# One copy of the 128-token chain behind each count of 192-token bodies; counting products in 64x64 blocks; the last copy over two engines

## The chip, the cores and the metric

The kernel runs on one core of one Trainium2 chip. The metric is the device time of one launch in microseconds (us), as the median of three runs.

## The reference

Sigmoid attention over 8 batches, 12 heads, 448 tokens and head size 64, then a mixture of 8 experts with one expert per token (3584 tokens, model width 768, hidden width 1024):

```python
scores = scale * np.matmul(q, k.transpose(0, 1, 3, 2)) - np.log(S)
attn = 1.0 / (1.0 + np.exp(-scores))
x = np.matmul(attn, v)                      # then (B*S, H*D)
logits = x @ w_gate
e_idx = np.argmax(logits, axis=1)
gate_w = softmax(logits)[np.arange(N), e_idx]
eom = 1.0 / (1.0 + np.exp(-(x @ w_output_gate)))
for e in range(E):
    mask = e_idx == e
    h = np.maximum(x[mask] @ w1[e], 0.0)
    out[mask] = gate_w[mask, None] * eom[mask, e, None] * (h @ w2[e])
```

## The kernel before, in words

**Attention** runs as 168 units (`attention`, from L858). A unit computes scores of 64 keys per head half (L898, matmuls on 64x64 blocks of TensorE), a sigmoid on ScalarE (L900) and, two units later, the products with v (L907, 64x64 blocks too), which gather in PSUM banks 4 to 7.

**Routing** (`route`) runs beside it for groups of 3, 2, 1, 1 and 1 batches. For each group it builds a one-hot matrix `oh` of tokens and experts and counts tokens: two TensorE products of 128x128 weights, `tri` for places within a chunk (L332) and `ones` for totals (L333). They go to one PSUM bank (`mm_ps`, bank 5; for the last group `mm_late`, bank 7), and ScalarE copies them out (L335). The counts give each token a row in the list of its expert, and GpSimd writes the lists by indirect DMA.

**Experts.** Each expert's tokens are cut into bodies: 256 tokens (`slot`), then a remainder as bodies of 192 (`wide_slot`) and of 128 tokens (`half_slot`). How many there are of each is known at run time only (`full`, `wide`, `part`, read at L1089 to L1091). A body multiplies its tokens by w1 (L644, L645, or L818 to L820 for 128 tokens), splits the hidden values in high and low parts, multiplies by w2 (L669 to L671), scales on ScalarE (L689, L850) and stores by indirect DMA (L691, L851). Weights of the next body are loaded by SyncE's queue (L587) and split by ScalarE (L600, L604) and VectorE (L601, L607).

The order of the bodies is written out by hand. The 256-token bodies behind the first are nested `If`s (L1102), the 192-token bodies a second nest (L1107), the 128-token bodies a chain (L1122 and L1127). Each nest leaves to one join, whatever its depth:

```python
for k in range(E):
    ctx.enter_context(tc.If(wide > k, label=f"wide{k}"))
    with tc.manual_schedule():
        self.wide_slot(k, hint("wide", wide, k, E))
```

`hint` marks, on TensorE alone, early in a body whether the next branch will be taken (a `BRANCH_PREFETCH_HINT`). Since the join can be reached from nine depths, each way out passes a landing block in which every engine waits for its own instructions and adds the counts of the bodies that did not run, so that all semaphores stand as if all had run; waits behind the join are against those sums. With the inputs timed here three 192-token and two 128-token bodies run.

The very last store is that of the last 128-token body: TensorE's second half of layer 2, ScalarE's scaled copy of 128x384 values (L850), the indirect DMA (L851).

Of the kernel before, what the change touches and what calls it, by code (L numbers as in the profile page):

```python
# [10 lines left out]
F32 = mybir.dt.float32  # L11
# [3 lines left out]
AF = mybir.ActivationFunctionType  # L15
ALU = mybir.AluOpType
# [7 lines left out]
E = 8  # L24
# [28 lines left out]
PLAIN = 6 * DF * 4 + 2 * XG + 8 * DM * 4  # L53


def r32(ap):
    return ap.bitcast(F32)


class Kernel:  # L60
# [20 lines left out]
    def memory(self):  # L81
        self.rounded = self.pool("rounded").tile([128, ROUNDED // 4], F32R, name="rounded")
        self.plain = self.pool("plain").tile([128, PLAIN // 4], F32, name="plain")
        ps = self.pool("psum", space=PSUM).tile([128, 8, 512], F32, name="ps")
        self.ps_s = [ps[:, 0:2], ps[:, 2:4]]
        self.ps_third = ps[:, 6:8]
        self.ps_o = [[ps[:, 4], ps[:, 5]], [ps[:, 6], ps[:, 7]]]
        self.mm_ps, self.mm_late = ps[:, 5], ps[:, 7]
        self.gp = ps[:, 6]
        self.psx = [ps[:, i].rearrange("p (d t) -> p d t", d=2) for i in (6, 7)]  # L90
        self.psh = [ps[:, i] for i in (0, 1, 2, 4, 5)]
        self.psy = [ps[:, i, 0:384] for i in (4, 5, 3, 6)]
        self.rot = {}

        c = self.carve
        w = c(0, 3, 2, 2, DF)
        self.w1s = [[w[:, d // 2, a, d % 2] for d in range(6)] for a in range(2)]
        self.w1p = [[w[:, k, a] for k in range(3)] for a in range(2)]
        self.xc = c(12 * DF * 4, 6, 2, TS)
        self.xs = [self.xc[:, :, i] for i in range(2)]  # L100

        self.w1r = c(0, 6, DF, dt=F32)
        o = 6 * DF * 4
        self.xg = c(o, 8, Q4, dt=F32)
        self.xT = c(o + XG, 6, TS, dt=F32)
        o += 2 * XG
        self.w2r = c(o, 8, DM, dt=F32)
        self.li = c(o, LROWS, 6, dt=F32)
        self.lr_e = [c(o + LROWS * 24 + i * 768, 192, dt=F32, parts=32) for i in range(2)]
        self.tmp_early = o + 4096  # L110
        self.step = c(o + 8192, B, 4, dt=F32)
        self.tokf = c(o + 8192 + 16 * B, NCH, 4, dt=F32)
# [146 lines left out]
    def route_tiles(self):  # L259
        rp, g = self.pool("route"), self.nc.gpsimd  # L260
        t = lambda n, shape, dt=F32: rp.tile(shape, dt, name=n)
        self.R, at = {}, [0]
        place = {3: 46080, 2: 53248}

        def early(name, dims):
            a = self.carve(at[0], *dims, dt=F32)
            at[0] += 4 * math.prod(dims)
            return a

        for k in sorted({n for _, n in GROUPS}):  # L270
            n = k * NCH
            at[0] = place.get(k)
            m = early if k > 1 else lambda name, dims: t(name, [128, *dims])
            R = self.R[k] = {
                name: m(name, dims)
                for name, dims in (("ahead", (E, n)), ("lg", (n, 32)), ("df", (n, E)), ("rk", (n, E)), ("sg", (3, n, E)),
                                   ("mf", (2, n)), ("t4", (n, 4)), ("t2", (n, 2)), ("posf", (n,)), ("den", (n,)),
                                   ("eom", (n,)), ("posi", (n,)), ("oh", (n * E // 2,)))}
            R["posi"] = R["posi"].bitcast(I32)
            R["oh"] = R["oh"].bitcast(BF16).rearrange("p (c e) -> p c e", e=E)  # L280
            lg = R["lg"].rearrange("p c x -> p (c x)")
            R["pc"], R["inc"], R["pos"] = (lg[:, n * E * i:n * E * j] for i, j in ((0, 2), (2, 3), (3, 4)))
            R["pos"] = R["pos"].rearrange("p (c e) -> p c e", e=E)
        g.memset(self.R[1]["ahead"], 1.0)
        g.memset(self.R[1]["ahead"][:, :, 0:1], 0.0)
        self.bad = t("bad", [128, NCH])
        for q in range(4):
            g.iota(self.bad[32 * q:32 * q + 32], pattern=[[32, NCH]], base=-QT, channel_multiplier=1,
                   allow_small_or_imprecise_dtypes=True)
        g.tensor_scalar(self.bad, self.bad, 0.0, float(OOB), ALU.is_ge, ALU.mult)  # L290
# [8 lines left out]
    def route(self, b, nb):  # L299
        nc = self.nc  # L300
        g, v = nc.gpsimd, nc.vector
        tt = g.tensor_tensor
        n = nb * NCH
        R = self.R[nb]
        mf, sg, pc, inc = R["mf"], R["sg"], R["pc"], R["inc"]
# [3 lines left out]
        by_c = lambda t: t.rearrange("p (c e) -> p c e", e=E)  # L309
        by_e = lambda t: t.rearrange("p (e c) -> p c e", e=E)  # L310
# [16 lines left out]
        oh = R["oh"]  # L327
        nc.scalar.activation(sg[:, 0], R["df"], AF.Sigmoid)
        nc.scalar.activation(sg[:, 1], R["df"], AF.Sigmoid, scale=-1.0)
        nc.scalar.activation(sg[:, 2], R["lg"][:, :, E:16], AF.Sigmoid)  # L330
        ps = self.mm_ps[:, 0:2 * n * E]
        nc.tensor.matmul(by_c(ps[:, 0:n * E]), self.tri, oh, start=True, stop=True)  # L332
        nc.tensor.matmul(by_e(ps[:, n * E:]), self.ones, oh, start=True, stop=True)  # L333
        yield "places"
        nc.scalar.copy(pc, ps)  # L335
        den = R["den"]
        v.reciprocal(sg[:, 1], sg[:, 1])
        v.tensor_tensor(sg[:, 0], sg[:, 0], sg[:, 1], ALU.mult)
# [412 lines left out]
            out_offset=bass.IndirectOffsetOnAxis(ap=s["lq"][:, 0:1], axis=0),  # L751
            in_=y[:, 0:384], in_offset=None, bounds_check=2 * NT - 1, oob_is_err=False)

    def wide_slot(self, j, hint):
        cur = self.wide_lists(j)
        if j:
            self.load_held()
        nx = self.load_slot(self.tab_l, LATE_F + j + 1, self.wide_lists(j + 1))
        self.nc.gpsimd.drain()
        self.split_w2(0)  # L760
        for f in range(8):
            if f == 6:
                self.finish()
            self.layer1(f, n=WS)
            if f == 0:
                hint()
            if f:
                self.high_low(f - 1, HS)
            if f in (1, 3, 5):
                self.split_w2(f // 2 + 1)  # L770
        self.high_low(7, HS)
        self.high_w1(0)
        self.turn_x(nx)
        self.gather(self.wide_lists(j + 2))
        for k in range(3):
            self.split_x(nx, k)
        self.low_w1(0)
        self.split_w1(1)
        self.split_w1(2)
        self.layer2_q(cur, self.ys[0])  # L780
        self.load_w2(nx, (0, 2, 4))
        self.layer2(cur, 0, 0, self.ys[1], self.psy[1])
        self.layer2_due(cur, 0)
        k = LATE_F + j + 1
        self.nc.vector.tensor_copy(self.held, self.tab_l[0:1, 0:3:2, k])

    def half_slot(self, j, last):
        nc = self.nc
        nx, y = None, self.ys[j % 2]
# [19 lines left out]
        for n in range(2):  # L809
            c = slice(512 * n, 512 * n + 512)  # L810
            ps = self.take("h", self.psh)
# [15 lines left out]
        cur = dict(lt=self.ltb[:, j])  # L827
        pss = self.psy[0:2]
# [15 lines left out]
        for n in range(2):  # L844
            self.layer2_mm(pss[n], 0, n, range(4, 8))
            if not last:
                self.layer2_out(pss[n], cur, 0, n, y)
                continue
            c = slice(384 * n, 384 * n + 384)
            nc.scalar.activation(y[:, c], pss[n], AF.Copy, scale=r32(cur["lt"][:, 0, 1:2]))  # L850
            nc.gpsimd.indirect_dma_start(  # L851
                out=self.outs[n].rearrange("t (n c) -> (t n) c", n=2),
                out_offset=bass.IndirectOffsetOnAxis(ap=self.lth[:, j, n:n + 1], axis=0),
                in_=y[:, c], in_offset=None, bounds_check=2 * NT - 1, oob_is_err=False)
# [165 lines left out]
    def build(self, phases="abc"):  # L1020
        tc, nc = self.tc, self.nc
# [65 lines left out]
        for m in range(EARLY + LATE_MIN):  # L1087
            if m == EARLY + LATE_MIN - 1:
                full = nc.values_load(self.tot[0:1, 0:1], min_val=0, max_val=LATE_MAX)  # L1089
                wide = nc.values_load(self.tot[0:1, 1:2], min_val=0, max_val=E)  # L1090
# [5 lines left out]
        def hint(name, n, k, end):  # L1096
            def mark():
                if k + 1 < end:
                    tc.mark_branch_hint_location(f"{name}{k + 1}", hint=n > k + 1, engines=[ET.PE])
            return mark  # L1100

        with ExitStack() as ctx:  # L1102
            for k in range(LATE_MIN, LATE_MAX):
                ctx.enter_context(tc.If(full > k, label=f"full{k}"))
                with tc.manual_schedule():
                    self.slot(EARLY + k, hint=hint("full", full, k, LATE_MAX))
        with ExitStack() as ctx:  # L1107
            for k in range(E):
                ctx.enter_context(tc.If(wide > k, label=f"wide{k}"))
                with tc.manual_schedule():  # L1110
                    self.wide_slot(k, hint("wide", wide, k, E))
        def body(k, last):
            with tc.manual_schedule():
                self.half_slot(k, last)
            if not last:
                halves(k + 1)
# [7 lines left out]
            with first.Else():  # L1124
                body(k, False)

        with tc.If(part > 1) as more:  # L1127
            body(0, False)
        with more.Else():
            with tc.If(part > 0) as one:  # L1130
                body(0, True)
            with one.Else():
                with tc.manual_schedule():
                    self.finish()


@with_exitstack
# [34 lines left out]
```

## Time and profile before

| | us |
|---|---|
| median of 3 runs (lowest, highest) | 765.19 (764.56, 765.5) |
| the profiled execution | 764.83 |
| its span, first to last instruction | 763.0 |
| TensorE busy (share of the span) | 755.0 (99%) |
| VectorE busy | 494.3 (65%) |
| ScalarE busy | 482.3 (63%) |
| GpSimd busy | 319.7 (42%) |

The profile is of one execution. PE is TensorE's array, PEld its weight loads, DVE VectorE, ACT ScalarE, POOL GpSimd, SP SyncE. A q behind a name (PEldq, ACTq) is that engine's instruction queue: branches, events and waits run there, and it may be ahead of the engine. Lines such as L818 are the kernel's. TensorE's granted clock is 0.998 of full over the span.

### The profile page before, as it was taken

What the parts mean: (1) busy time and instruction counts of PE and PEld (TensorE: products, weight loads), DVE (VectorE), ACT (ScalarE), POOL (GpSimd) and SP (SyncE); (2) the same over time, 40 slices, a digit from 0 to 9 for tenths busy, and PEclk for the clock granted to TensorE, in tenths of its full rate; (3) what the DMA queues carried; (4) which work ended last, traced back from release to release, by engine and by line L of the source; (5) the groups of instructions that cost most, each with busy time, mean ns of one, the idle gap of its engine ahead of it and who ended that gap; (6) DMA issues with size and microseconds to landing.
All of it is one profiled execution on the core that took longest, in us unless ns stands there. A gap on an engine that the chain in (4) does not pass through costs nothing. (4 is left out here: it accounts for less than half of the span.)

```text
span 763.0 us, 15197 instructions
## 1 busy us (share of the span) xinstructions
PE 755.0 (99%) x5775; PEld 591.2 (77%) x5775; DVE 494.3 (65%) x918; ACT 482.3 (63%) x643; POOL 319.7 (42%) x400
## 2 busy tenths in 40 slices
PE   9999999999999999999999999999999999999996
PEld 5777754444434489899999999999999999889786
DVE  3333344345477579888887866858576685877783
ACT  5666657666687756566565665757566574675683
POOL 5000005502446477883643727255372734524611
PEclk9999999999999999999999999999999999999999
DMA  7463544536486450238857768511156856488691
GB/s 262 143 218 137 198 174 146 176 118 219 138 320 250 115 178 10 76 90 339 287 188 270 247 212 294 160 52 43 42 189 216 297 158 220 165 291 296 216 383 60
DMA packets 43648, 144.82 MB, mean 190 GB/s; under 512 B 5623, under 2 KB 7839, under 8 KB 42528
## 3 DMA queue, kind: packets, MB, share of 16 engines
q1 hardware_dynamic: 33872, 119.56, 44.9%
q0 software_dynamic: 9680, 24.07, 9.3%
q8 instruction: 49, 0.80, 0.4%
q14 instruction: 47, 0.39, 0.2%
HBM read 145.93 MB, written 23.06 MB: 221 GB/s over the span
## 5 line engine op out<-in xcount | busy, mean ns | idle before, releaser
L644 PE MATMUL ps<-rounded 128*128 128x512 f32 (+1 forms) x672 | 225.7, 385 | 0.7 <-PEq L1102 0.7
L900 ACT ACTIVATE a<-ps,bias_s 128x896 f32<-128x896 f32 x168 | 169.1, 1007 | 87.0 <-PE ps L898 86.4
L564 POOL DMA_INDIRECT plain<-x_dram,lxs x122 | 182.5, 1496 | 93.3 <-DVE plain L626 54.6
L898 PE MATMUL ps<-kqv 64*64 64x448 f32 x1344 | 193.9, 542 | 0.0
L907 PE MATMUL ps<-a,kqv 64*64 64x448 f32 x1344 | 192.1, 536 | 0.0
L645 PE MATMUL ps<-rounded 128*128 128x256 f32 (+1 forms) x672 | 183.9, 274 | 0.0
L669 PE MATMUL ps<-w2h,h 128*128 128x384 f32 x432 | 145.0, 336 | 0.0
L671 PE MATMUL ps<-w2h,h 128*128 128x384 f32 x432 | 144.5, 334 | 0.0
L670 PE MATMUL ps<-w2l,h 128*128 128x384 f32 x432 | 144.5, 334 | 0.0
L601 DVE TENSOR_TENSOR w2l<-plain,w2h 128x1536 fp32r<-128x1536 f32 x60 | 105.2, 1756 | 60.5 <-ACT w2h L600 60.5
L644 PEld LDWEIGHTS ps<-rounded 128*128 128x128 f32 x672 | 125.8, 187 | 23.6 <-issue 1.8
L645 PEld LDWEIGHTS ps<-rounded 128*128 128x128 f32 x672 | 127.3, 189 | 0.0
L898 PEld LDWEIGHTS ps<-kqv 64*64 64x64 f32 x1344 | 66.5, 134 | 60.0 <-issue 41.8
L907 PEld LDWEIGHTS ps<-a,kqv 64*64 64x64 f32 x1344 | 67.3, 133 | 57.8 <-issue 45.1
L607 DVE TENSOR_TENSOR rounded<-plain,rounded 128x2048 fp32r<-128x2048 f32 x44 | 98.9, 2285 | 2.9 <-ACT rounded L604 2.9
L652 ACT COPY gl<-ps 128x256 f32<-128x256 f32 (+1 forms) x112 | 40.4, 360 | 95.3 <-PE ps L645 89.5
L600 ACT CAST w2h<-plain 128x1536 fp32r<-128x1536 f32 x60 | 88.0, 1469 | 17.8 <-PE ps L943 4.8
L604 ACT CAST rounded<-plain 128x2048 fp32r<-128x2048 f32 x44 | 83.4, 1902 | 0.0
L669 PEld LDWEIGHTS ps<-w2h,h 128*128 128x128 f32 x432 | 81.1, 188 | 2.3 <-issue 1.8
L670 PEld LDWEIGHTS ps<-w2l,h 128*128 128x128 f32 x432 | 81.1, 188 | 0.1
L671 PEld LDWEIGHTS ps<-w2h,h 128*128 128x128 f32 x432 | 81.1, 188 | 0.0
L691 POOL DMA_INDIRECT out<-y,due x11 | 20.0, 1814 | 126.3 <-ACT gl L652 116.1
(259 smaller groups left out, 663.8 us busy)
## 6 DMA issues: line engine op xcount, KB each, us to landing
plain<-w SPq DMA_DIRECT2D x64, 768.0 KB
plain<-w SPq DMA_DIRECT2D x45, 1024.0 KB
kqv<-kqv SPq DMA_DIRECT2D x23, 1344.0 KB
x_dram<-xt SPq DMA_DIRECT2D x8, 1344.0 KB
plain<-w SPq DMA_DIRECT2D x6, 512.0 KB
plain<-x_dram,lxs POOLq DMA_INDIRECT x122, 5.3
kqv<-kqv SPq DMA_DIRECT2D x2, 448.0 KB
lst<-plain POOLq DMA_DIRECT2D x1, 726.0 KB
```

The costliest lines, as they stand in the source:

```text
L564: self.nc.gpsimd.indirect_dma_start(out=s["xg"][:, g], out_offset=None, in_=x4, in_offset=bass.IndirectOffsetOnAxis(ap=s["lx"][:, g:g + 1] ...
L600: self.nc.scalar.copy(hi, raw)
L601: self.nc.vector.tensor_tensor(lo, raw, r32(hi), ALU.subtract)
L607: self.nc.vector.tensor_tensor(self.w1p[1][k], self.w1r[:, 2 * k:2 * k + 2], r32(self.w1p[0][k]), ALU.subtract)
L644: nc.tensor.matmul(out, wh[d][:, c], both, start=(d == 0), stop=False)
L645: nc.tensor.matmul(ps[:, 0:n], wl[d][:, c], self.xc[:, d, 0, 0:n], start=False, stop=(d == 5))
L669: nc.tensor.matmul(ps, hh[:, f, tk], wh, start=(f == 0), stop=False)
L670: nc.tensor.matmul(ps, hh[:, f, tk], wl, start=False, stop=False)
L671: nc.tensor.matmul(ps, hl[:, f, tk], wh, start=False, stop=(f == 7))
L898: nc.tensor.matmul(ps[half[h], j, 0:S], kg[half[j], e, 1, o:o + 64], kg[half[j], e, 0], start=True, stop=True)
L900: nc.scalar.activation(at[u % 4], ps[:, :, 0:S], AF.Sigmoid, bias=self.bias_s, scale=1.0 / math.sqrt(D))
L907: nc.tensor.matmul(self.ps_o[e][h][half[j], 0:S], v[half[h], 6 if i == 3 else 3 * e + c, j], a[half[h], j], start=(i in ((0, 3 if h else 4 ...
```

## The change

Three things. First, the chain of 128-token bodies (now `after`) is written nine times: once behind each of the eight 192-token bodies, where the count ends there, and once for no such body. A 192-token body ends with a branch on the count; where it falls through, the chain stands next, and where it is taken, the next 192-token body stands behind the whole chain. The join and its landing blocks are gone between the two, and so is the hint in `wide_slot`. Second, the two counting products of a group become eight products of 64x64 blocks in two PSUM banks, one per half of the tokens; ScalarE copies both banks out and VectorE adds them. The last group keeps one bank and two products. Third, in the last 128-token body the copy of the second 384 columns is made half by ScalarE, half by VectorE.

```diff
-        self.mm_ps, self.mm_late = ps[:, 5], ps[:, 7]
+        self.mm_ps, self.mm_late = ps[:, 4:6], ps[:, 7:8]
...
+            w = 2 * n * E
+            R["pp"] = early("pp", (2, w)) if k > 1 else self.carve(PLAIN - 8 * w, 2, w, dt=F32)
...
-        ps = self.mm_ps[:, 0:2 * n * E]
-        nc.tensor.matmul(by_c(ps[:, 0:n * E]), self.tri, oh, start=True, stop=True)
-        nc.tensor.matmul(by_e(ps[:, n * E:]), self.ones, oh, start=True, stop=True)
+        w = 2 * n * E
+        ps = self.mm_ps[:, :, 0:w]
+        half = [slice(0, 64), slice(64, 128)] if ps.shape[1] == 2 else [slice(0, 128)]
+        blocks = [(m, i, k) for m in half for i, k in enumerate(half)]
+        for m, i, k in blocks:
+            nc.tensor.matmul(by_c(ps[m, i, 0:n * E]), self.tri[k, m], oh[k], start=True, stop=True)
+        for m, i, k in blocks:
+            nc.tensor.matmul(by_e(ps[m, i, n * E:]), self.ones[k, m], oh[k], start=True, stop=True)
         yield "places"
-        nc.scalar.copy(pc, ps)
+        if len(half) == 1:
+            nc.scalar.copy(pc, ps[:, 0])
+        else:
+            nc.scalar.copy(R["pp"], ps)
+            v.tensor_tensor(pc, R["pp"][:, 0], R["pp"][:, 1], ALU.add)
...
-    def wide_slot(self, j, hint):
+    def wide_slot(self, j):
...
-            if f == 0:
-                hint()
...
-            nc.scalar.activation(y[:, c], pss[n], AF.Copy, scale=r32(cur["lt"][:, 0, 1:2]))
+            w = r32(cur["lt"][:, 0, 1:2])
+            if n == 0:
+                nc.scalar.activation(y[:, c], pss[n], AF.Copy, scale=w)
+            else:
+                nc.scalar.activation(y[:, 384:576], pss[n][:, 0:192], AF.Copy, scale=w)
+                nc.vector.tensor_scalar(y[:, 576:768], pss[n][:, 192:384], w, None, ALU.mult)
...
-        with ExitStack() as ctx:
-            for k in range(E):
-                ctx.enter_context(tc.If(wide > k, label=f"wide{k}"))
-                with tc.manual_schedule():
-                    self.wide_slot(k, hint("wide", wide, k, E))
...
+        def wides(k):
+            with tc.manual_schedule():
+                self.wide_slot(k)
+            if k == E - 1:
+                after()
+                return
+            with tc.If(wide < k + 2) as done:
+                after()
+            with done.Else():
+                wides(k + 1)
+
+        with tc.If(wide > 0) as some:
+            wides(0)
+        with some.Else():
+            after()
```

**Place 1: TensorE, from the second 192-token body to the third, and out to the chain.** In the rows a `MATMUL` carries its weight load; `w2h`, `w2l` and `h` are layer 2's operands, `rounded` layer 1's; a name with 49 is the semaphore of that engine. Before, body to body:

```order
4064 L669 MATMUL ps<-w2h,h_2529 128x384
4065 L670 MATMUL ps<-w2l_2536,h_2529 128x384
4066 L671 MATMUL ps<-w2h,h_2530 128x384
4067 L1107 COMPARE_AND_BRANCH
4068 L644 MATMUL ps<-rounded 128x384 [waits DVE_49,Activation_49]
4069 L645 MATMUL ps<-rounded 128x192 [waits DVE_49]
```

Before, out of the nest (the eight landing blocks, then the chain):

```order
4868 L670 MATMUL ps<-w2l_2536,h_2529 128x384
4869 L671 MATMUL ps<-w2h,h_2530 128x384
4870 L1107 UNCONDITIONAL_BRANCH
4871 L1107 UNCONDITIONAL_BRANCH [waits PE_49] x8
4872 L1127 COMPARE_AND_BRANCH
4873 L818 MATMUL ps<-rounded 128x512 [waits DVE_49,Activation_49]
4874 L819 MATMUL ps<-rounded 128x512 [waits DVE_49]
```

Now, the end of a 192-token body (here the first): the chain is next,

```order
3785 L681 MATMUL ps<-w2l_2564,h_2557 128x384
3786 L682 MATMUL ps<-w2h,h_2558 128x384
3787 L1152 COMPARE_AND_BRANCH
3788 L1137 COMPARE_AND_BRANCH
3789 L827 MATMUL ps<-rounded 128x512 [waits Activation_49]
3790 L828 MATMUL ps<-rounded 128x512 [waits DVE_49]
```

and the target of L1152, the next 192-token body, stands behind the copy:

```order
5125 L681 MATMUL ps<-w2l_2564,h_2557 128x384
5126 L682 MATMUL ps<-w2h,h_2558 128x384
5127 L1140 UNCONDITIONAL_BRANCH
5128 L1140 UNCONDITIONAL_BRANCH [waits PE_49]
5129 L655 MATMUL ps<-rounded 128x384 [waits DVE_49,Activation_49]
5130 L656 MATMUL ps<-rounded 128x192 [waits DVE_49]
```

The landing blocks have left the way from body to chain; the way from body to body has become a jump from row 3787 to row 5129.

**Place 2: VectorE at the end of the last 128-token body.** In the copy behind three 192-token bodies; `h` is the hidden values, `w2l` the low part of w2, `y` the output rows. Before:

```order
1152 L601 TENSOR_TENSOR h_2530<-ps,h_2529 128x4x128 [waits Activation_49]
1153 L808 TENSOR_TENSOR w2l_2536<-plain,w2h 128x1536 [waits DMAHW2_49]
1154 L808 TENSOR_TENSOR w2l_2536<-plain,w2h 128x1536 [waits DMAHW3_49,Activation_49]
1155 L601 TENSOR_TENSOR h_2530<-ps,h_2529 128x4x128 [waits Activation_49]
1156 L1122 UNCONDITIONAL_BRANCH
```

Now:

```order
1289 L612 TENSOR_TENSOR h_2558<-ps,h_2557 128x4x128 [waits Activation_49]
1290 L817 TENSOR_TENSOR w2l_2564<-plain,w2h 128x1536 [waits DMAHW6_49]
1291 L817 TENSOR_TENSOR w2l_2564<-plain,w2h 128x1536 [waits DMAHW7_49,Activation_49]
1292 L612 TENSOR_TENSOR h_2558<-ps,h_2557 128x4x128 [waits Activation_49]
1293 L864 TENSOR_SCALAR y_2566<-ps,gl_113 128x192 [waits DMASW2_49,Activation_49]
1294 L1131 UNCONDITIONAL_BRANCH
```

VectorE's half of the last copy (L864) reads the same PSUM bank as ScalarE's half (L863) and waits for ScalarE's count; the last store waits for VectorE's.

## Rows read from the trace of the kernel before

**Rows 1.** Busy time by stretch: us, busy of PE, PEld, DVE, ACT, POOL; clock; DMA.
```profile
721.00:740.00 19.00, 18.33 (x97) 16.56 (x96) 13.72 (x12) 14.87 (x17) 2.95 (x3) 1.00 0.88 315
```

**Rows 2.** Timeline of PE at the way out: start, us, line, shape, idle and releaser.
```profile
720.85 0.34 PE L671 MATMUL ps<-w2h,h 128*128 128x384 f32 x1
721.86 0.47 PE L818 MATMUL ps<-rounded 128*128 128x512 f32 x1 [0.67 <-ACTq L1107]
```

**Rows 3.** Timeline of PE, from 192-token body to body.
```profile
666.05 0.34 PE L644 MATMUL ps<-rounded 128*128 128x384 f32 x1
...
693.36 0.34 PE L671 MATMUL ps<-w2h,h 128*128 128x384 f32 x1
693.53 0.34 PE L644 MATMUL ps<-rounded 128*128 128x384 f32 x1
```

**Rows 4.** Line L1107 in the queues, 716 to 722: ns min/median/max, first and last start.
```profile
L1107 ACTq COMPARE_BRANCH  x2: 38/44/50, 717.1 to 721.5; - x2
L1107 PEldq COMPARE_BRANCH  x2: 192/276/361, 717.9 to 721.4; - x2
...
L1107 PEldq EVENT_SEMAPHORE  x1: 51/51/51, 721.2 to 721.2; - x1
L1107 ACTq EVENT_SEMAPHORE  x1: 17/17/17, 721.4 to 721.4; - x1
```

**Rows 5.** Line L1107 in TensorE's queue, 660 to 664 and 688 to 692.
```profile
L1107 PEldq COMPARE_BRANCH  x1: 68/68/68, 662.9 to 662.9; - x1
...
L1107 PEldq COMPARE_BRANCH  x1: 68/68/68, 690.4 to 690.4; - x1
```

**Rows 6.** Lines L1122 and L1168 (the end) in the queues, from 750.
```profile
L1122 PEldq COMPARE_BRANCH  x1: 3412/3412/3412, 753.9 to 753.9; - x1
L1122 ACTq COMPARE_BRANCH  x1: 38/38/38, 757.3 to 757.3; - x1
...
L1168 ACTq DRAIN  x2: 8/37/66, 760.1 to 762.5; - x2
```

**Rows 7.** Busy time by stretch: single microseconds behind branches.
```profile
663.00:664.00 1.00, 1.00 (x8) 1.00 (x7) 1.00 (x1) 0.88 (x1) 0.71 (x1) 1.00 0.31 109
...
690.00:691.00 1.00, 1.00 (x8) 1.00 (x7) 1.00 (x2) 0.55 (x2) 1.00 (x1) 1.00 1.08 387
...
717.00:718.00 1.00, 1.00 (x8) 1.00 (x7) 1.00 (x2) 0.59 (x1) 1.00 (x1) 1.00 1.03 404
```

**Rows 8.** Timeline of PE around the first counting products.
```profile
112.97 0.93 PE L898 MATMUL ps<-kqv 64*64 64x448 f32 x8
113.72 0.93 PE L907 MATMUL ps<-a,kqv 64*64 64x448 f32 x8
114.59 0.22 PE L332 MATMUL ps<-plain,tri 128*128 128x96 bf16 x1
...
114.82 0.98 PE L898 MATMUL ps<-kqv 64*64 64x448 f32 x8
```

**Rows 9.** Timeline of PEld (weight loads) there.
```profile
113.72 0.15 PEld L907 LDWEIGHTS ps<-a,kqv 64*64 64x64 f32 x4 [0.22 <-issue]
114.58 0.10 PEld L332 LDWEIGHTS <-tri 128*128 128x128 bf16 x1 [0.71 <-issue]
```

**Rows 10.** Timeline of ACT there.
```profile
115.58 0.32 ACT L335 COPY plain<-ps 128x192 f32<-128x192 f32 x1
...
117.37 1.01 ACT L900 ACTIVATE a<-ps,bias_s 128x896 f32<-128x896 f32 x1 [0.49 <-PE ps L898]
```

**Rows 11.** Timeline of the last copy.
```profile
757.25 0.58 ACT L850 ACTIVATE y<-ps,gl 128x384 f32<-128x384 f32 x1 [1.56 <-PE ps L671]
```

**Rows 12.** Groups by line and shape, 690 to 764: busy us, mean ns, idle before.
```profile
L653 DVE TENSOR_TENSOR gl<-gl,ps 128x192 f32<-128x192 f32 x8 | 2.8, 347 | 2.9 <-ACT gl L652 2.9
L652 ACT COPY gl<-ps 128x192 f32<-128x192 f32 x8 | 2.5, 316 | 6.4 <-PE ps L645 4.8 <-ACT h L657 1.6
```

**Rows 13.** Timeline of DVE at the end of the second 192-token body.
```profile
687.99 4.49 DVE L607 TENSOR_TENSOR rounded<-plain,rounded 128x2048 fp32r<-128x2048 f32 x2
```

More of the change, by code (lines that the diff above doesn't have):

```diff
@@ L1125, in halves, with after @@
                 body(k, False)
[L1127 to L1134, printed above, removed]
+        def after():
+            with tc.If(part > 1) as more:
+                body(0, False)
+            with more.Else():
+                with tc.If(part > 0) as one:
+                    body(0, True)
+                with one.Else():
+                    with tc.manual_schedule():
+                        self.finish()
+        def wides(k):
+            with tc.manual_schedule():
+                self.wide_slot(k)
[10 more added lines that the diff above has]
+            after()
 @with_exitstack
```

## Prediction, made before the change was run

> **What bounds the kernel now.** I read the busy time by stretch first. Over the step from the 192-token bodies into the 128-token ones, and the first of those, TensorE is busy 18.33 of 19.00 us [rows 1], and the only gap in it is the step itself [rows 2]. So whatever keeps TensorE waiting there is paid in full, and whatever moves on another engine is free as long as TensorE's next matmul does not need it. Four things are touched: the branch between 192-token bodies, the branch out of them, the counting products inside attention, and the last copy.
>
> **Which path runs.** The trace shows three 192-token bodies and two 128-token bodies: three L1107 branches that fall into a body and a fourth that leaves, and then L818 matmuls. Of the nine copies only the one behind the third body runs. To reach it, all five engines now jump over the copy behind the first body, then over the copy behind the second; after the third they fall straight in. Before, two falls and one jump out.
>
> **The branch out (removed).** TensorE's last 192-token matmul starts at 720.85, the first L818 at 721.86 [rows 2]: 1.01 us from start to start, where the step from body to body takes 0.17 (693.36 to 693.53) [rows 3]. So the exit costs 0.84 us. The queue view says of what: the landing block holds an event in which TensorE's queue waits for all its own matmuls (721.2) and adds the counts of the bodies not run, then a branch of 192 ns; only then does it reach L818 [rows 4]. ACT's landing event is as late, at 721.4, 4.3 us after ACT's branch at 717.1 [rows 4], and the waits list names it for TensorE's gap [rows 2]. In the new order the row behind the body's last matmul is the chain's first, and it waits for ScalarE's split alone, the next row for VectorE's: ordinary operands, which the waits list does not name here. I take the whole **-0.84**. If nothing came back it would be 0; a gain above 1.01 is excluded.
>
> **The two jumps (added).** Between bodies TensorE's queue met its branch at 662.9 and at 690.4, each for 68 ns, falling through [rows 5]; the next body's first matmul started at 666.05 and 693.53 [rows 3]. The queue is thus 3.1 us ahead of the array, and a stall there is bare only beyond 3.1 us. The change makes both branches jumps, over about 1,340 printed TensorE rows, and drops their prefetch hint. What an unhinted jump takes on TensorE the trace shows once: the branch to the program's end at 753.9 holds the queue 3412 ns [rows 6]. The hinted jump out took 361 at most [rows 4]. From a landing to the array there are some 0.2 us more (721.4 and its 192 ns, then 721.86 [rows 2, 4]). So a jump that takes F costs F + 0.2 - 3.1: at F = 3.41, 0.5 us.
>
> But 3.41 was seen with the DMA engines idle. ScalarE gives the price of load: its jump at 757.3 was followed by its next instruction at 760.1, 2.8 us [rows 6]; its jump at 717.1, with DMA share 1.03 in that microsecond, by 4.3 [rows 4, 7], 1.5 more. The two new jumps fall at the end of a weight load: share 0.31 just behind 662.9, and 1.08 in the microsecond that holds 690.4 [rows 7]. My estimate, from ScalarE's 1.5 in proportion to the load met, is F = 3.7 and 4.1, so 0.8 + 1.2 = **+2.0**. The bounds: 0 (a fetch of 2.9 or less, as ScalarE's 2.8, stays under the lead) and 4.0 (3.41 + 1.5 = 4.9 each).
>
> [...]
>
> The other engines jump too. VectorE is in the body's last two splits until 692.5 [rows 13], with the branch behind them already taken by its queue. ScalarE's first work after the jump, the split of w2, is for layer 2 at the body's far end. SyncE next waits for a value that VectorE writes as the body's last act. GpSimd is still issuing the gathers. All four are hidden. If that cover were gone, VectorE would be late next: it empties layer 1's PSUM banks, three deep, and TensorE would stand at the fourth tile of the body.
>
> **The counting products.** In attention eight matmuls follow eight every 0.75 us, so after L907 at 113.72 scores would start at 114.47; with counting they start at 114.82 [rows 8]: 0.35 us for the first call. The loading of `tri` waits until 114.58, 0.71 us after the load before it; in the usual rhythm the idle is 0.22 [rows 9]. That looks like the array emptying between 64x64 and 128x128 use, which the blocks avoid. Four calls are changed (the fifth keeps one bank and its two products); the other three move fewer columns, so I take 0.35 as their most: 1.4 us in all. The blocks have their own price: two sets of four weight loads, each set 0.15 us [rows 9], under products too short to hide them, so 0.30 per call; part of the first set hides under the attention matmuls, I take 0.27. That is 4 x -0.08 = **-0.3**. Bounds: -1.4 (all hidden) and +0.4 (three sets bare, the attention set behind them included: 0.45).
>
> ScalarE copies twice the columns, at most 0.58 instead of 0.32 us, against an idle of 0.49 per unit [rows 10, 11]; VectorE adds one sum of at most 0.35 us [rows 12], whose results GpSimd waits for and TensorE does not. Zero.
>
> **The last copy.** It is now 0.58 us on ScalarE [rows 11]. Split over two engines that ran together it would be 0.35. But the order shows VectorE's half waiting for ScalarE, and the store waiting for VectorE: the halves follow each other. By the nearest rows, a PSUM read of 128x192 is 0.32 on ScalarE and 0.35 on VectorE [rows 12], so 0.67 and a hand-over of 0.04: **+0.13**. Bounds -0.23 and +0.25. [...]
>
> **Sum.** -0.84 + 2.0 - 0.3 + 0.13 = +1.0 us on the profiled execution, 764.83 (763.0 span and 1.8 around it), so 765.8. The median shown, 765.19, is 0.36 above the profiled one; on that scale **766.2**.
>
> **Rivals.**
> 1. *Slower: loaded fetches.* Place: the two jumps on TensorE. If weights in flight cost it what they cost ScalarE, F = 4.9, each jump 2.0: -0.84 + 4.0 - 0.3 + 0.13 = +3.0, **768.2**. It decides once F averages 4.2. For it: the 4.3 on ScalarE, and three other engines jumping in the 2 us before TensorE. Against: the load ends within a microsecond of either jump. Chance 0.25.
> 2. *Slower a little: the exit gives nothing back*, because the queue stands at the new entry for something else (the copy exists but does not do what it is for): +1.8, 767.0. Against: the named wait is gone from the order. Chance 0.07.
> 3. *Slower by much: nothing covers the fetch.* The queue's lead is spent, each jump is bare for 3.41 + 0.2: 7.2 - 1.0 = +6.2, 771.4. The rows show the lead at both branches. [...] Chance 0.05.
> 4. *Faster: the jumps hide.* F at 2.9 or less, and the blocks cost 0.1 a call: -0.84 - 1.0 + 0.13 = -1.7, 763.5. For it: ScalarE's quiet 2.8; against: TensorE's own 3.41. Chance 0.10.
>
> **How the numbers follow.** A measurement of this kernel tells about 0.2% (1.5 us) from no change, so 763.7 to 766.7 counts as the same. My forecast, a net of +1.0 out of terms of both signs, lies inside: 0.53. Faster is rival 4, 0.10; slower is 1 to 3, 0.37. The range reaches from the near side of rival 4, 764.0, to just past rival 1, 769.0; rival 3 and the far side of 4 are left out.
>
> **What would show it.** Right: no gap between the last 192-token matmul and the chain's first; TensorE's queue branches near 663 and 690 lasting 3.4 to 4.3 us, each with a gap of 0.5 to 1.4 us in front of the next body; attention's counting step below 0.35 us; VectorE's half starting only when ScalarE's ends. Wrong: gaps of 2 us or more at the jumps (rival 1), of 3.6 (rival 3), or none (rival 4); a gap that stays at the entry (rival 2).

## The result, and the profile after

The changed kernel takes 773.89 us (median of 6 runs, 772.10 to 774.85); the kernel before took 764.63 us beside it (6 runs). The ratio is 1.0115, 95% interval 1.0105 to 1.0125: slower by 1.15%. The prediction was 766.2 us, with a range from 764.0 to 769.0. It was wrong, and the range did not hold the time.

The profiled executions took 774.85 and 764.83 us, with spans of 772.8 and 763.0: 9.8 us apart. (The first is the slowest of its six; the medians lie 9.3 us apart.) TensorE has almost no gaps in this part of the kernel, so the difference can be read off as the time from the start of one matmul to the start of another. Lines have moved in the changed kernel: layer 1 of a 192-token body is L655 and L656 (L644 and L645 before), layer 2 is L680 to L682, the chain's layer 1 is L827 to L829, and the branch between 192-token bodies is L1152.

| stretch on TensorE | before, us | after, us | difference |
|---|---|---|---|
| span's start to the first 192-token matmul | 638.50 | 637.61 | -0.89 |
| step from body 1 to body 2 (jump 1) | 0.18 | 0.65 | +0.47 |
| step from body 2 to body 3 (jump 2) | 0.17 | 1.85 | +1.68 |
| layer 1 of body 3, first matmul to last | 13.55 | 22.00 | +8.45 |
| step from body 3 into the chain | 1.01 | 0.17 | -0.84 |
| the chain, first matmul to last | 34.95 | 35.90 | +0.95 |
| last matmul to the end of the span | 6.19 | 6.11 | -0.08 |
| rest of the three bodies | | | +0.06 |

Their sum is +9.8. Before, layer 1 of body 3 ran from 693.53 [rows 3] to this row of the timeline of PE of the kernel before (start, us, line, shape):

```profile
707.08 0.25 PE L645 MATMUL ps<-rounded 128*128 128x192 f32 x1
```

The same timeline of the changed kernel, at the two jumps and the end of that layer, which answers to [rows 3]:

```profile
637.61 0.41 PE L655 MATMUL ps<-rounded 128*128 128x384 f32 x1 [0.68 <-PEq L1116]
...
665.00 0.34 PE L682 MATMUL ps<-w2h,h 128*128 128x384 f32 x1
665.65 0.41 PE L655 MATMUL ps<-rounded 128*128 128x384 f32 x1 [0.31 <-issue]
...
693.02 0.34 PE L682 MATMUL ps<-w2h,h 128*128 128x384 f32 x1
694.87 0.41 PE L655 MATMUL ps<-rounded 128*128 128x384 f32 x1 [1.52 <-issue]
701.41 0.53 PE L656 MATMUL ps<-rounded 128*128 128x192 f32 x1 [6.13 <-issue]
701.73 0.58 PE L655 MATMUL ps<-rounded 128*128 128x384 f32 x1
...
716.87 0.25 PE L656 MATMUL ps<-rounded 128*128 128x192 f32 x1
```

Two things stand out. The two jumps leave idle times of 0.31 and 1.52 us, of the kind forecast. Behind the second one, a single matmul runs, and then TensorE stands for 6.13 us. The releaser is "issue": nothing that the profile shows held it. After that an L655 matmul takes 0.58 us, where it is 0.36 in the first jump's body.

Line L1152 in TensorE's queue, in three windows (ns min/median/max, first and last start), answers to [rows 5]. The branches that fell through in 68 ns now hold the queue for the jump, and the third falls into the chain:

```profile
L1152 PEldq COMPARE_BRANCH  x1: 3406/3406/3406, 662.1 to 662.1; - x1
...
L1152 PEldq COMPARE_BRANCH  x1: 4611/4611/4611, 690.1 to 690.1; - x1
...
L1152 PEldq COMPARE_BRANCH  x1: 70/70/70, 727.7 to 727.7; - x1
```

Busy time by stretch around the second jump (us; busy of PE, PEld, DVE, ACT, POOL with counts; PE's granted clock; DMA share; GB/s):

```profile
694.00:696.00 2.00, 0.41 (x1) 0.19 (x1) 0.00 (x0) 0.99 (x1) 1.25 (x2) 1.00 0.62 105
696.00:698.00 2.00, 0.00 (x0) 0.00 (x0) 1.49 (x1) 0.48 (x1) 0.00 (x0) 1.00 0.95 262
698.00:700.00 2.00, 0.00 (x0) 0.00 (x0) 0.27 (x1) 0.00 (x0) 0.00 (x0) 0.71 1.03 391
700.00:702.00 2.00, 0.59 (x2) 0.59 (x3) 0.00 (x0) 0.00 (x0) 0.00 (x0) 0.50 1.02 415
702.00:704.00 2.00, 2.00 (x9) 2.00 (x9) 0.00 (x0) 0.00 (x0) 0.00 (x0) 0.50 1.01 408
704.00:706.00 2.00, 2.00 (x10) 2.00 (x10) 0.35 (x1) 0.32 (x1) 0.00 (x0) 0.58 1.03 414
706.00:708.00 2.00, 2.00 (x16) 2.00 (x15) 0.66 (x3) 1.03 (x3) 0.00 (x0) 1.00 0.44 170
```

While TensorE stands, the weights of the next body fill the DMA engines (share 0.95 to 1.03), and its granted clock falls from 1.00 to 0.50. It is back at 1.00 in the stretch from 706. So the +8.45 us are the idle 6.13, and some 2.3 of work at half clock.

What TensorE waited for is in the rows of the DMA queues. One queue, q8, carries 0.87 MB of instructions in 53 packets, 16.4 KB each; before it was 49. I take it for TensorE's, since its packets follow TensorE's branches. The q8 rows (packets, MB, share of 16 engines' span) of the whole span, of 690.0 to 691.7, of 691.7 to 693.4 and of 698.7 to 700.2:

```profile
q8 instruction: 53, 0.87, 0.5%
...
q8 instruction: 1, 0.02, 4.3%
...
q8 instruction: 1, 0.02, 6.0%
...
q8 instruction: 1, 0.02, 5.7%
```

Between 693.4 and 698.7 there is none. The first jump's rows, of 662.1 to 665.5 (while its branch holds the queue) and of 665.5 to 668.2:

```profile
q8 instruction: 1, 0.02, 2.0%
...
q8 instruction: 1, 0.02, 4.0%
```

There one packet comes while the branch holds the queue, and one behind the landing. At the second jump two come while the branch holds it (690.1 to 694.7), and the one behind the landing is late. So a block of instructions came up to 693.4, TensorE started at 694.87, the next block came between 698.7 and 700.2, and TensorE went on at 701.41. That is the reading that the experiments test: the jump landed at the very end of a block, and the block behind it had yet to be fetched through full DMA queues.

The other rows that answer to those of before, all from the timeline. The step into the chain, for [rows 2]:

```profile
730.62 0.34 PE L682 MATMUL ps<-w2h,h 128*128 128x384 f32 x1
730.79 0.39 PE L827 MATMUL ps<-rounded 128*128 128x512 f32 x1
```

The first counting products, for [rows 8]: the next attention matmul, due at 114.51 by the rhythm of 0.75 us, starts at 114.59, so the call costs 0.08 us where it cost 0.35.

```profile
113.76 0.93 PE L921 MATMUL ps<-a,kqv 64*64 64x448 f32 x8
114.51 0.22 PE L338 MATMUL ps<-plain,tri 64*64 64x96 bf16 x4
114.55 0.26 PE L340 MATMUL ps<-plain,ones 64*64 64x96 bf16 x4
114.59 0.97 PE L912 MATMUL ps<-kqv 64*64 64x448 f32 x8
```

The last copy, for [rows 11]: VectorE's half waits for ScalarE's, and the last store starts 1.15 us after ScalarE began (before, by 757.25 and a store at 758.10, 0.85).

```profile
767.12 0.42 ACT L863 ACTIVATE y<-ps,gl 128x192 f32<-128x192 f32 x1 [1.56 <-PE ps L682]
767.58 0.42 DVE L864 TENSOR_SCALAR y<-ps,gl 128x192 f32<-128x192 f32 x1 [6.44 <-ACT y L863]
768.27 0.97 POOL L865 DMA_INDIRECT out<-y,gl  x1 [1.47 <-DVE y L864]
```

And the +0.95 us in the chain are one wait in its last body, where ScalarE's split of w2 came late:

```profile
759.08 0.66 PE L812 MATMUL ps<-ident,hb 128*128 128x128 f32 x4 [0.76 <-ACT hb L833]
```

### The profile page after: what moved, and what is told of

It is laid out like the page before. It is cut to its first block, busy times and chain, and to the rows that moved or that the text cites. A ratio compares the mean times of both kernels' runs of the same rounds, so it can differ in the third digit from the quotient of the medians.

```text
span 772.8 us, 15202 instructions
## 1 busy us (share of the span) xinstructions
PE 756.8 (98%) x5799; PEld 582.2 (75%) x5799; DVE 495.5 (64%) x923; ACT 481.7 (62%) x643; POOL 320.7 (41%) x400
## 5 line engine op out<-in xcount | busy, mean ns | idle before, releaser
L655 PE MATMUL ps<-rounded 128*128 128x512 f32 (+1 forms) x672 | 227.8, 388 | 2.5 <-issue 1.8
L656 PE MATMUL ps<-rounded 128*128 128x256 f32 (+1 forms) x672 | 185.0, 275 | 6.1 <-issue 6.1
L655 PEld LDWEIGHTS ps<-rounded 128*128 128x128 f32 x672 | 127.0, 189 | 26.1 <-issue 4.3
L680 PE MATMUL ps<-w2h,h 128*128 128x384 f32 x432 | 145.0, 336 | 0.0
L682 PE MATMUL ps<-w2h,h 128*128 128x384 f32 x432 | 144.5, 335 | 0.0
L656 PEld LDWEIGHTS ps<-rounded 128*128 128x128 f32 x672 | 128.4, 191 | 6.4 <-issue 6.4
L680 PEld LDWEIGHTS ps<-w2h,h 128*128 128x128 f32 x432 | 81.1, 188 | 2.3 <-issue 1.8
L682 PEld LDWEIGHTS ps<-w2h,h 128*128 128x128 f32 x432 | 81.1, 188 | 0.0
```

Of the source, the lines that this page charges most:

```text
L655: nc.tensor.matmul(out, wh[d][:, c], both, start=(d == 0), stop=False)
L656: nc.tensor.matmul(ps[:, 0:n], wl[d][:, c], self.xc[:, d, 0, 0:n], start=False, stop=(d == 5))
L680: nc.tensor.matmul(ps, hh[:, f, tk], wh, start=(f == 0), stop=False)
L682: nc.tensor.matmul(ps, hl[:, f, tk], wh, start=False, stop=(f == 7))
```

## The experiments

The runs fell on three chips, on which the kernel before took 764.7 to 764.9 us (runs 1 to 4, 11 and 12), 767.0 us (5 to 7) and 766.7 us (8 to 10). So ratios to the kernel before, taken beside each run, are compared, and not times. Theory A is the one above: what cost the 8.45 us in layer 1 of body 3 is the place in a block where the second jump lands.

### 1 and 2. Move the landing by half a block

Instructions are added where no token count of this input comes: behind the last `finish()` of one copy of the chain, which runs only when there are no 128-token bodies at all. They shift the addresses of what lies behind, and nothing else. In run 1 they are in the second copy, which the second jump crosses; in run 2 in the first, which the first jump crosses.

```
-        def after():
+        def after(copy=None):
...
                     with tc.manual_schedule():
                         self.finish()
+                        if copy == 1:
+                            for _ in range(64):
+                                nc.tensor.matmul(self.mm_late[:, 0, 0:64], self.ones, self.ones[:, 0:64], start=True, stop=True)
...
             with tc.If(wide < k + 2) as done:
-                after()
+                after(k)
```

> The changed kernel with 64 products (128 TensorE instructions) added in a branch that no token count here takes, in the second copy of the chain. No instruction that runs is touched; only the address of the third 192-token body, where the second jump lands, moves by 128. Theory A (the 6.1 us stop one matmul after the second landing is the fetch of the next block of instructions, which came due at once because the landing lies at the end of a block, and the half clock behind it follows from the stop): no stop behind the second landing, full clock, 773.9 - 6.1 - 2.0 = 765.8 us. Rival B (the stop belongs to the body or to the weights that fill the DMA queues there, wherever the code lies): the 6.1 us stay, 773.9 us. Rival C (any unhinted jump is followed by such a stop, only its length varies): a stop of 3 to 6 us stays, 769 to 774 us.

> The same 128 instructions in the first copy of the chain: both landings move by 128, the distance between them is as in the changed kernel. Theory A: no stop behind the second landing; behind the first one only if its new place is the end of a block; 765.8 us, at most 2 us more with a stop in the first, where the DMA queues are a third full. Rival B: stop behind the second landing as before, 773.9 us. Rival C: 769 to 774 us.

Measured: 766.62 us, a ratio of 1.0024 (1.0014 to 1.0033), and 766.09 us, 1.0017 (1.0008 to 1.0027). In both, no stop is left behind either landing, and the mean granted clock is 0.999 (0.994 in the changed kernel). Rival B falls: body, weights and waits are the same, and 7 to 7.5 us are gone. Rival C falls with it.

### 3. The hints put back

```
             self.layer1(f, n=WS)
+            if f == 0:
+                hint()
...
+                    tc.mark_branch_hint_location(f"wide{k + 1}", hint=wide < k + 2, engines=[ET.PE])
...
-            with tc.If(wide < k + 2) as done:
+            with tc.If(wide < k + 2, label=f"wide{k + 1}") as done:
```

> The changed kernel with TensorE's hint put back into every 192-token body but the last, on the branch to the next body. Rival D (the missing hint is all of it): both jumps lose under 0.3 us, no stop, full clock: 773.9 - 0.5 - 1.7 - 6.1 - 2.0 = 763.6 us. Theory A: the two jumps lose less, up to 2.2 us, and the stop behind the second stays unless the 2 instructions that each hint adds (4 before the second landing) carry the landing over the block's end: 771.7 us with the stop, 763.6 us without it, and then the place of the stop, not the jump, tells the two apart.

Measured: 764.24 us, a ratio of 0.9996 (0.9987 to 1.0005). The branch to the next body (now L1160) in TensorE's queue, and the timeline of PE at the second jump:

```profile
L1160 PEldq COMPARE_BRANCH  x1: 355/355/355, 661.4 to 661.4; - x1
...
L1160 PEldq COMPARE_BRANCH  x1: 2492/2492/2492, 688.9 to 688.9; - x1
```

```profile
691.79 0.34 PE L682 MATMUL ps<-w2h,h 128*128 128x384 f32 x1
691.97 0.34 PE L655 MATMUL ps<-rounded 128*128 128x384 f32 x1
```

With its hint, neither jump costs anything: 355 and 2492 ns both lie under the queue's lead of 3.1 us, and the step is 0.18 us, as between bodies that follow each other. That the stop is gone too does not speak for the hint: its 4 added instructions move the second landing by 4, and run 5 shows what 8 do.

### 4. The blocks alone

The part of the change on counting, in the kernel before.

> The kernel before with only the counting products as four blocks. By the trace of the changed kernel, whose first 192-token body began 0.9 us earlier: 764.6 - 0.9 = 763.7 us. By the prediction's term: 764.6 - 0.3 = 764.3 us. Rival (the 0.9 us came from the code layout ahead of the body): 764.6 us.

Measured: 763.74 us, a ratio of 0.9989 (0.9980 to 0.9998), 0.93 us below the kernel before: the size read from the trace of the changed kernel, three times the prediction's.

### 5 to 7. Where does the block end?

The same edit with 4 products (8 instructions) and 120 products (240) in the second copy, and with 20 products (40) in the first.

> The changed kernel with only 8 TensorE instructions (4 products) added in the never-taken branch of the second copy: the second landing moves by 8 instructions. Theory A in its sharp form (one matmul ran before the stop, so the block of instructions ends within a few instructions of the landing; a landing 8 further on lies at the start of the next block, 250 instructions from its end): no stop behind the second landing, full clock, 766.2 us. Rival (what heals is a shift by a large part of a block, or chance, not the end of the block): the stop stays, 772 to 774 us.

> 240 instructions in the same branch. An instruction block is 16384 bytes in the DMA rows of the trace; at 64 bytes each that is 256 instructions, so the second landing lies 16 instructions nearer the start of its block than in the changed kernel. Theory A: some 18 instructions run behind the landing before the stop, about 1.2 us at 4 instructions in 0.285 us, so a stop of 6.1 - 1.2 = 4.9 us, the half clock behind it as before, 772.7 us. Rival (any large shift heals): no stop, 766.2 us.

> 40 instructions in the never-taken branch of the first copy. The two landings lie 3112 instructions apart by the program, 12 blocks of 256 and 40, so the first landing now takes the place in its block that the second had, and the second one moves on by 40. Theory A: no stop behind the second landing; one behind the first, and shorter, since the DMA queues are a third full there: in the changed kernel the next block's fetch ended 2.4 us after the first matmul, and execution follows a fetch by 1.3 us: a stop of about 3.5 us, with up to 2 us of half clock behind it: 769.7 to 771.7 us. Rival B (the stop needs the full DMA queues of the second jump, the place alone does nothing): no stop at either, 766.2 us. Rival (the stop belongs to the second jump wherever it lands): 773.9 us.

Run 5: 766.98 us, a ratio of 1.0006 (0.9995 to 1.0016). Eight instructions that never run, and the stop is gone. The timeline of PE behind its second jump:

```profile
692.95 0.34 PE L682 MATMUL ps<-w2h,h 128*128 128x384 f32 x1
694.45 0.41 PE L655 MATMUL ps<-rounded 128*128 128x384 f32 x1 [1.16 <-issue]
694.70 0.25 PE L656 MATMUL ps<-rounded 128*128 128x192 f32 x1
```

Run 6: 772.32 us, a ratio of 1.0066 (1.0040 to 1.0092). The stop is back, later and shorter:

```profile
695.59 0.41 PE L655 MATMUL ps<-rounded 128*128 128x384 f32 x1 [1.28 <-issue]
...
696.78 0.36 PE L655 MATMUL ps<-rounded 128*128 128x384 f32 x1
701.93 0.32 PE L656 MATMUL ps<-rounded 128*128 128x192 f32 x1 [4.80 <-issue]
```

Nine matmuls run before it, where one ran in the changed kernel: 8 matmuls, each with its weight load, are 16 instructions more. So 240 instructions brought the landing 16 places nearer the start of its block, as they would if a block is 240 + 16 = 256 instructions long. The end of the block did not move, the landing did. Forecast was a stop of 4.9 us, and it is 4.80 in the profiled execution. That one is the slowest of four (773.96 us, the lowest 770.82). The forecast time, 772.7 us, was a ratio of 1.0105 to the kernel before as run 1 had it, so by the ratio the median came out some 3 us below it; the profile of one execution does not show by what. The half clock follows it here too (busy time by stretch, two of the stretches):

```profile
702.00:704.00 2.00, 2.00 (x8) 2.00 (x8) 0.35 (x1) 0.32 (x1) 0.00 (x0) 0.50 1.01 410
...
708.00:710.00 2.00, 2.00 (x15) 2.00 (x15) 2.00 (x3) 0.53 (x2) 0.00 (x0) 1.00 0.06 23
```

The kernel before shows the same length: from 14.3 to 592.6 us q8 brings 37 packets, while TensorE runs 4699 matmuls and 4692 weight loads, 254 instructions for each packet of 16.4 KB, those of its queue not counted. At 256 a packet that is the 64 bytes an instruction that the expectation took.

Run 7: 767.03 us, a ratio of 1.0000 (0.9990 to 1.0010). Here half of my expectation failed. Behind the first landing there is a stop, but a small one, and after 17 matmuls rather than one:

```profile
666.46 0.41 PE L655 MATMUL ps<-rounded 128*128 128x384 f32 x1 [0.35 <-issue]
...
668.84 0.36 PE L655 MATMUL ps<-rounded 128*128 128x384 f32 x1
669.65 0.25 PE L656 MATMUL ps<-rounded 128*128 128x192 f32 x1 [0.46 <-issue]
```

So the first landing was some 35 instructions from a block's end, not 3: my count of the distance between the landings was off by 32, and the code that I counted is not quite the code that is loaded. But the run gives the price of the next block at a lighter load: the stop ends 3.2 us after the landing's first matmul (666.46 to 669.65, with a mean DMA share of 0.65). It was 6.5 us in the changed kernel (694.87 to 701.41, share 0.98) and 6.3 in run 6 (695.59 to 701.93, share 0.97). What is bare of it (0.46, 6.13 and 4.80 us) is what the instructions left in the block do not fill.

The load alone does not settle how late the next block comes. In run 5 the second landing lies 0.4 us earlier than in the changed kernel, before the same weights, and its q8 row of 694.25 to 695.3 already has the next packet:

```profile
q8 instruction: 1, 0.02, 10.0%
```

The changed kernel has none up to 698.7, 4 us behind its landing. In both, the first packets of those weights (q1) come between 695.2 and 695.6. That the fetch came before the weights in one and behind them in the other is my reading; whether the landing's place in the block also holds the fetch back, no run separates.

### 8. The split of the last copy alone

The part of the change on the last copy, in the kernel before.

> The kernel before with only the last copy split between ScalarE and VectorE. By the trace of the changed kernel the two halves run one behind the other (0.42 us, then 0.42 us from 0.46 us after the first began) and the last store is issued 1.58 us after the last matmul began, 1.29 us before: +0.3 us. The prediction's term: +0.13 us. Rival (the halves overlap, as the edit would have it): -0.2 us. Against the kernel before a ratio of 1.0004, 1.0002 or 0.9997: at the edge of what can be told, the trace's tail decides.

Measured: 766.29 us against 766.74, a ratio of 0.9995 (0.9986 to 1.0004): nothing to be told. The trace's tail is as in the changed kernel:

```profile
758.64 0.42 ACT L854 ACTIVATE y<-ps,gl 128x192 f32<-128x192 f32 x1 [1.56 <-PE ps L671]
759.10 0.42 DVE L855 TENSOR_SCALAR y<-ps,gl 128x192 f32<-128x192 f32 x1 [6.13 <-ACT y L854]
```

From the last matmul's start to the span's end it took 5.9 us here, 6.2 before, 5.8 and 6.5 in two profiles of the blocks alone. The end scatters by more than the split's 0.3 us on the store, so whether that reaches the end is left open.

### 9 to 12. The nest turned, and the price of its parts

Run 9 keeps the blocks and leaves the last copy whole. The next 192-token body is now what follows in the code; each body's own copy of the chain is the else side, and TensorE's hint is on the branch as before.

```
+            with tc.If(wide > k + 1, label=f"wide{k + 1}") as more:
+                wides(k + 1)
+            with more.Else():
+                after()
```

Run 10 is run 3 without the split.

> Blocks kept, last copy not split, and the nest turned: the next 192-token body is the code that follows, with TensorE's hint on its branch, and each body's own copy of the chain is the else side, so one jump, hinted, is left and no join. Theory A: bodies follow each other without a fetch at a jump, the way out loses nothing as in the kernel with hints: blocks alone less the 0.8 us of its way out, a ratio of 0.9978 to the kernel before (762.9 us where that takes 764.6). Rival (the far jump is as late as the one with joins): 0.9988, as blocks alone. Rival (its landing meets the end of a block, with a stop of up to 5 us): 1.003 or more.

> The kernel with hints without the split of the last copy. If the split costs 0.3 us as the tail of the traces has it: a ratio of 0.9992 to the kernel before, against 0.9996 with the split. If the split is free or better: 0.9996 or more.

> Blocks alone once more, on the same chip as the turned nest, because the kernel before has taken 764.7 us on one chip and 766.7 to 767.0 us on others: a ratio to the kernel before of 0.9989 as before, if the 0.9 us are the counting products'.

> The turned nest with the blocks, beside blocks alone. If its way out gives back the 0.77 us of idle TensorE: 0.8 us below blocks alone, 0.9978 of the kernel before. If the ratio of 0.9962 measured on the other chip is its real size: 2 us below blocks alone. If nothing is given back: as blocks alone.

| run | us | ratio to before | interval |
|---|---|---|---|
| 9, nest turned | 763.94 | 0.9962 | 0.9949 to 0.9975 |
| 10, hints, no split | 764.72 | 0.9980 | 0.9969 to 0.9991 |
| 11, blocks alone | 763.79 | 0.9985 | 0.9976 to 0.9994 |
| 12, nest turned | 762.57 | 0.9972 | 0.9960 to 0.9984 |

Run 9 came out below its forecast of 0.9978, and run 12 near it. Beside each other on one chip, the turned nest is 1.2 us below blocks alone. The timeline of PE at the way out in run 11, and in run 12:

```profile
719.92 0.34 PE L682 MATMUL ps<-w2h,h 128*128 128x384 f32 x1
720.92 0.47 PE L829 MATMUL ps<-rounded 128*128 128x512 f32 x1 [0.67 <-PEq L1118]
```

```profile
719.88 0.34 PE L682 MATMUL ps<-w2h,h 128*128 128x384 f32 x1
720.05 0.39 PE L829 MATMUL ps<-rounded 128*128 128x512 f32 x1
```

1.00 us from start to start has become 0.17, across one hinted jump. That is 0.83 of the 1.2; the rest lies within the intervals. In run 12 TensorE is busy for 117.30 of the 117.30 us from 638.0 to 755.3, from the first 192-token body to the end of the chain. This version beats both kernels: 762.57 us against 764.88 for the kernel before. It has one landing for each token count, and a landing near a block's end could cost it the stop as well; here it does not.

Run 10's ratio is 0.0016 below run 3's (1.2 us), against 0.0004 expected for the split, but on another chip, so that difference is not put down to the split.

## Why the prediction was wrong

**The way out: right.** 0.84 us were to come back, and 1.01 became 0.17, exactly that.

**The jumps: the price of a fetch right, its length by luck.** The rule was that a jump of F costs F + 0.2 - 3.1. The changed kernel's two jumps took 3.41 and 4.61 us, which by the rule is 0.5 and 1.7, and they cost 0.47 and 1.68. The forecast had F at 3.7 and 4.1, and a sum of 2.0 against 2.15.

That the sums are close is luck, since F does not follow the load, from which it was forecast. (The working is off as well: in proportion to the shares of [rows 7], the 1.5 us would give an F of 3.9 and 5.0.) Run 7's second branch, its microsecond, and its q8 row of 691.6 to 695.1, while the branch holds the queue:

```profile
L1155 PEldq COMPARE_BRANCH  x1: 3492/3492/3492, 691.6 to 691.6; - x1
...
691.00:692.00 1.00, 1.00 (x8) 1.00 (x7) 1.00 (x2) 0.31 (x1) 1.00 (x1) 1.00 1.03 390
...
q8 instruction: 1, 0.02, 2.0%
```

At a share of 1.03 the fetch took 3.49 us, hardly more than the 3.41 with the DMA engines idle; the 4.61 us came at 0.98. What F goes with is the number of q8 packets that start while the branch holds the queue. With one, in both jumps of runs 2 and 7, both of run 1 and the first of the other three kernels, F is 3.35 to 3.75 us. With two, in the second jump of the changed kernel and of runs 5 and 6, it is 4.25 to 4.61. What the packet in front brings is not shown.

**The step that failed** is "So a jump that takes F costs F + 0.2 - 3.1": it took a landing for the end of the matter. At both jumps the code went on in a next block, whose packet started only behind the landing, at 666.3 us (first matmul at 665.65) and at 698.7 (694.87). For the wait for that next block the sum had no term, and layer 1 of body 3 grew by 8.45 us. How soon that one is needed went with where in the block the jump lands: after one matmul in the changed kernel, after nine in run 6, and after 17 at the first jump of run 7. In the changed kernel the queue's lead was spent and the weights filled the DMA engines (a share of 0.95 to 1.03): 6.13 us idle, then some 2.3 at half clock. None of the rivals had it. Rival 3 has a time nearer to the result, 771.4, but says that nothing covers the fetch, and the fetch of the landing block was covered by 3.1 us in both jumps. The prediction counted the rows that a jump crosses, and didn't ask where in a block it lands; that instructions come in packets of 16 KB (49 packets, 0.80 MB on q8) stood in the page of before.

With the landing moved off the block's end, the ratio is 1.0024, 1.0017, 1.0006 and 1.0000 in runs 1, 2, 5 and 7. The predicted sum of +1.0 us is 1.0013. This is close in part by luck: without the 8.45 us the table leaves +1.35, in which the counting products (-0.89 before the bodies, where -0.3 was taken) and the chain (+0.95, where nothing was) partly cancel.

**The blocks: right in sign, too small.** -0.3 was taken, -0.93 and -1.09 us were measured. The term that was mis-sized is the price of the blocks' own weight loads, 0.27 us per call: the first call costs 0.08 us in all, so most of the two sets is hidden. The other three, read in the same way from the two timelines, cost 0.07, 0.06 and 0.06 us, where it was 0.31, 0.28 and 0.28: 0.95 us over the four. The idle time in front of the load of `tri`, 0.71 us before [rows 9], is 0.22 with the blocks (the load starts at 114.14): the wait that the prediction put down to the change between 64x64 and 128x128 use is gone.

**The last copy: the order of the halves was right.** VectorE's half does start only behind ScalarE's. The halves took 0.42 us each where 0.32 and 0.35 were taken from a plain copy and an addition, so the store starts 0.3 us later, and not 0.13; in the time it can't be told.

**Not foreseen, and not settled:** the wait of 0.76 us in the chain's last body, where ScalarE splits the last piece of w2 late. The step there is longer than its usual 0.18 us in 6 of the 8 profiled kernels whose 192-token bodies have copies of the chain between them (by 0.2 to 1.1 us), and by no more than 0.04 in the 6 whose bodies follow each other. A later arrival of that weight piece would explain it; why it is later was not tried.

## What to carry to other kernels

Code that doesn't run can have a price by its length: it moves what lies behind it, and here 8 instructions more of it made a ratio of 1.0115 one of 1.0006. Where a jump is needed, put the hot path in the code that follows and hint the branch (a step of 0.17 us in run 12, where the unhinted jumps of the changed kernel took 0.65 and 1.85), and look behind each landing for a gap with the releaser "issue", 6.13 us here; if one is there, a few instructions of padding show whether the place is its cause. A loss that appears without a named releaser, in work that is the same as before, is first to be looked for in the rows of the instruction queues.

## What was not expected of the hardware

Eight instructions that never run decide over some 8 us: a ratio to the kernel before of 1.0115 without them, of 1.0006 with them. The block behind a landing was usable 3.2 us after the landing's first matmul at a mean DMA share of 0.65, and 6.3 to 6.5 us after it at 0.97 and 0.98, where no packet of q8 came for 4 us. An unhinted jump held TensorE's queue for 3.35 to 3.75 us with one instruction packet in that time (once at a share of 1.03), and for 4.25 to 4.61 us with two. In a stop of 4.8 or 6.1 us the granted clock fell to 0.50, which cost some 2 us more in the changed kernel; in the idle times of up to 1.5 us at the jumps it stayed at 1.00.
